# Attention, first group: the inversion in blocks of 16x16 on DVE, joined by small products on PE

## The chip, the cores and the metric

The kernel runs on one core of a Trainium2 chip. The metric is the time of one execution on the device in microseconds; of several executions the median is taken. In the text PE is TensorE (PEld its weight loads), DVE VectorE, ACT ScalarE, POOL GpSimd and SP the queue that issues most DMAs.

## The reference, cut to what matters

Three parts follow one another: a linear attention with a state, a routed feed-forward layer with eight experts, and a dense feed-forward layer. The change is in the first.

```python
for t in range(S):                              # S = 768; B, H, D = 4, 8, 40
    y[:, :, t] = einsum('bhd,bhde->bhe', rt, state)
    Sa = einsum('bhde,bhe->bhd', state, at)
    state = state * wt[:, :, None, :] - einsum('bhd,bhe->bhde', Sa, bt)
    state = state + einsum('bhd,bhe->bhde', vt, kt)
...
x = y as 3072 rows of 320
x = gate * relu(x @ w1[e]) @ w2[e]              # e: the expert with the largest logit of the row
out = g(x @ w_in) @ w_out                       # g: a leaky relu, 2048 wide
```

## The kernel before, in words

**Tiling.** Attention works in chunks of 64 steps. Inside a chunk the recurrence becomes products of matrices, once the inverse of a unit lower triangular 64x64 matrix is known, one for each chunk and head. A group is 4 chunks (256 steps) of 16 heads (two of the four batches); there are six groups. A group's 64 matrices lie as two on top of each other on the 128 partitions, for 4 chunks `c` and 8 pairs of heads `u`; the tile `l2` [128, 4, 8, 32] holds their diagonal blocks of 32x32, one in each quarter of 32 partitions, and `l1` the blocks below the diagonal.

**The inverse** (`inverse`, L529 to L614) is a generator; whoever calls `next` sets off the instructions up to the next `yield`. First DVE transposes `l2` into `ul` (L536), so that each partition holds one block of 32x32 in its free dimension: 128 blocks side by side. Then it inverts all of them by columns: for each of 31 columns `j` a product of column and row into `tmp` (L554) and a subtract from `ut` (L556), on (31-j)(j+1) elements in each partition. In the first group (`o.start`) `ut` lies in PSUM (`unit_start`) and `tmp` in SBUF; in the others `ut` lies in SBUF and `tmp` in the PSUM bank `mg`, into which ACT also copies parts of `ul` (L551). After that DVE transposes `ut` back, once as `ttc` and once as `t11` (L576, L579), and `diagonal` puts the inverted blocks on the diagonal of `tt` (L572; in the first group on DVE for the first half, else on POOL). For each half of the group (two chunks) PE then joins blocks of 32 to 64: a product of `l1` with the inverted blocks into `zp` (L600), a copy to `z` on ACT (L604), a product with `t11` into `yp` (L610), a copy with the sign into `tt` (L613). Ahead of `zp` and `yp` of the first group eight products of ones (`fill`) are issued. `zp` and `yp` take the one bank `mg`, except in the second half of the later groups. `check` (L590, L591) sums squares on ACT, with `ut` and `ttc` as the places of the unwanted output.

**Buffers.** `t4` is a ring of three tiles of 128x1024 in SBUF that all of this shares, in the order of the calls: in the first group four `junk` tiles, `ul`, `tmp`, `ttc`, `t11`; in each later one `ut` (cleared by POOL, L368), `ul`, `ttc`, `t11`. A tile that comes round again waits for the last reader of its buffer.

**Stages and order.** `prepare` (L440) loads a quarter of a group and forms two scans and a reciprocal on DVE (L467 to L469) and scaled operands (`kb`, L472; `abd`, L476); `products` (L479) multiplies them (`lp`, L497), copies `l1` and `l2` on ACT and `la` on DVE (L505); POOL at the end of each half copies parts of `l1` into `l2` (L504). `sides` (L509) transposes the operands on PE (L517, L521) with copies on ACT. `run` (L737) calls these for the first group in an order written out by hand; then come `rest` (clears), the inverse of the first group as far as the second half's checks (L805 to L807), and `prepare` and `products` of the second group. From there 48 slots follow, one for each chunk of two batches, which carry the state on, and each group's work is laid some slots ahead; the second group's inverse begins in slot 0, its matrices are needed in slot 8. Within the region of L316 the order on DVE, POOL and ACT is as written; behind it a planner chooses the order of each engine's instructions, and it always does so for PE. Each engine carries out its list in that order.

Of the kernel before, what the change touches and what calls it, by code (L numbers as in the profile page):

```python
# [9 lines left out]
F32 = mybir.dt.float32  # L10
# [5 lines left out]
ALU = mybir.AluOpType  # L16
# [4 lines left out]
P = 128  # L21
# [216 lines left out]
def whole(gen):  # L238
    for _ in gen:
        pass  # L240
# [45 lines left out]
NCS = SL // C  # L286
# [4 lines left out]
class Attention:  # L291
# [234 lines left out]
    def t4(self, nm):  # L526
        return self.pa.tile([P, NCS, 8, 32], F32, name=nm, tag="t4", bufs=3)

    def inverse(self, o):  # L529

        nc = self.nc
        l1, l2 = o.l1, o.l2
        o.tt = [self.ringed("tt", self.tt) for _ in range(2)]
        ut = self.ut0 if o.start else self.unit()
        ul = self.pa.tile([P, 32, 32], F32, name="ul", tag="t4", bufs=3)
        nc.vector.transpose(ul, l2.rearrange("p c u j -> p j (c u)"))  # L536
        yield
        for j in range(31):
            n, m = 31 - j, j + 1
            if o.start:  # L540
                if j == 0:
                    tmp = self.pa.tile([P, 1024], F32, name="tmp", tag="t4", bufs=3)
                col = ul[:, j, j + 1:]
            else:
                if j == 0:
                    bank = self.work("tmp", [P, 512], "mg")
                    tmp = bank[:, :256]
                if j in (0, 8, 16):
                    j0, j1 = j, (8, 16, 32)[j // 8]
                    part = bank[:, 256:256 + (j1 - j0) * (32 - j0)].rearrange("p (a b) -> p a b", b=32 - j0)  # L550
                    nc.scalar.copy(part, ul[:, j0:j1, j0:])  # L551
                col = part[:, j - j0, j + 1 - j0:]
            tv = tmp[:, :n * m].rearrange("p (a b) -> p a b", b=m)
            nc.vector.tensor_tensor(tv, col.unsqueeze(2).to_broadcast([P, n, m]),  # L554
                                    ut[:, j, :m].unsqueeze(1).to_broadcast([P, n, m]), op=ALU.mult)
            nc.vector.tensor_tensor(ut[:, j + 1:, :m], ut[:, j + 1:, :m], tv, op=ALU.subtract)  # L556
            if j % 2:
                yield
# [9 lines left out]
        def diagonal(half):  # L568
            for q in (1, 3, 0, 2):
                r = slice(32 * q, 32 * q + 32)  # L570
                eng = nc.vector if o.start and half == 0 else nc.gpsimd
                eng.tensor_scalar(o.tt[half][r, :, :, 32 * q:32 * q + 32], ttc[r, 2 * half:2 * half + 2], 1.0, 0.0, op0=ALU.mult, op1=ALU.add)  # L572

        vacant(0)
        ttc = self.t4("ttc")
        nc.vector.transpose(ttc.rearrange("p c u t -> p t (c u)"), ut)  # L576
        diagonal(0)
        t11 = self.t4("t11")
        nc.vector.transpose(t11.rearrange("p c u s -> p s (c u)"), ut.rearrange("p t s -> p s t"))  # L579
        yield  # L580

        pairs = [(c2, u) for u in range(8) for c2 in range(2)]
# [3 lines left out]
        for half in range(2):  # L586
            if half:
                vacant(1)
                diagonal(1)
                self.check(ut, ut, 0.01)  # L590
                self.check(l1.rearrange("p c u j -> p (c u) j"), ttc.rearrange("p c u t -> p (c u) t"), 0.01)  # L591
                yield
            tt = o.tt[half]
# [143 lines left out]
    def run(self, rt, sp, moe, ctx):  # L737
        tc, nc = self.tc, self.nc
        os = []
        for bp in range(B // 2):  # L740
            for g in range(S // SL):
                o = K()
# [42 lines left out]
        o = os[0]  # L785
# [10 lines left out]
        inv = self.inverse(o)  # L796
# [5 lines left out]
        self.count["kb"] = self.count["abd"] = 0  # L802
        with tc.issue_after(o.last_v.ins), tc.issue_after(o.last_s.ins), tc.issue_after(o.last_g.ins):
            whole(self.rest())
        for _ in range(17):  # L805
            next(inv)
        next(inv)  # L807
        self.slots_room()
        at(0, 0, lambda: whole(inv))
        with tc.issue_after(o.last_v.ins), tc.issue_after(o.last_s.ins), tc.issue_after(o.last_g.ins):  # L810
# [638 lines left out]
```

## Time and profile before

| | us |
|---|---|
| median of three runs (lowest, highest) | 1068.68 (1065.76, 1071.46) |
| the profiled execution | 1070.7 |
| its span, first to last instruction | 1068.9 |
| PE busy in the span | 972.1 |
| PEld | 867.7 |
| DVE | 682.3 |
| ACT | 537.0 |
| POOL | 479.6 |

Busy time is a mean over stages with different limits; attention ends near 470 us and the feed-forward layers fill the rest. The mean granted clock of PE was 0.965 of full speed. A chain of waits follows the work back from what ended last: each piece is released by the one before.

### The profile page before, as it was taken

To read this page: it belongs to the slowest core of one execution; us is meant where nothing else is said; L and a number is where in the kernel's file an instruction comes from. 1 tells how busy PE (TensorE), PEld (TensorE's weight loads), DVE (VectorE), ACT (ScalarE), POOL (GpSimd) and SP (SyncE) were. 2 spreads that over 40 slices of the span, in tenths; PEclk is the share of its full clock that TensorE was granted. 3 is DMA by queue.
4 is the path that set the end of the run, shared out by engine and by line. 5 is a ranking of instruction groups with operands and counts; after the bars stand their busy time and mean duration, and the time that the engine had idled before them with its cause. 6 is when DMAs were issued, how large, how long until landed. Compare 5 with 4: busy or idle time off the path is not lost.

```text
span 1068.9 us, 24462 instructions
## 1 busy us (share of the span) xinstructions
PE 972.1 (91%) x9311; PEld 867.7 (81%) x9311; DVE 682.3 (64%) x1440; ACT 537.0 (50%) x1315; POOL 479.6 (45%) x576
## 2 busy tenths in 40 slices
PE   3668988899889988888999999999999999999997
PEld 2557867787678877778999999988989988988896
DVE  8785987968869695566687776644534454444433
ACT  4556867686677868655566655521312122222211
POOL 6756687886977645420000000034334343435332
PEclk8658999999999999999999999999999999999999
DMA  4372333333333234627788865610000000100000
GB/s 122 83 230 55 90 79 86 95 76 98 91 76 87 55 71 108 184 70 230 223 266 254 258 190 177 186 41 26 25 2 25 25 25 25 26 26 25 25 1 28
DMA packets 126048, 103.34 MB, mean 97 GB/s; under 512 B 90596, under 2 KB 108004, under 8 KB 125924
## 3 DMA queue, kind: packets, MB, share of 16 engines
q1 hardware_dynamic: 122596, 89.90, 29.9%
q0 software_dynamic: 3328, 11.80, 3.5%
q8 instruction: 76, 1.25, 0.5%
q14 instruction: 48, 0.39, 0.1%
HBM read 79.39 MB, written 22.28 MB: 95 GB/s over the span
## 4 chain that ended last, share of the span: by engine, by line
PE 66%; DVE 17%; issue 5%; ACT 4%; DMA 4%; POOL 3%; SPq 0%; another core or an unknown queue 0%; POOLq 0%; DVEq 0%; ACTq 0%
PE ph L244 26%; PE po L244 24%; DVE tmp L554 3%; DVE ut L556 3%; PE lp L497 2%; DVE s L467 2%; DVE q L469 2%; PE tr_ps L272 2%; PE sa L692 2%; DVE va L697 2%; PE pp L652 2%; PE yc L708 1%; PE ap L521 1%; PE rvp L663 1%; PE xp L244 1%
## 5 line engine op out<-in xcount | busy, mean ns | idle before, releaser
L235 POOL TENSOR_TENSOR gl<-g,gh 128x512 fp32r<-128x512 f32 x96 | 123.9, 1294 | 211.0 <-ACT gh L234 120.5
L234 ACT ACTIVATE gh<-g 128x512 fp32r<-128x512 f32 x96 | 60.7, 632 | 253.0 <-DVE g L1336 174.9
L1335 DVE TENSOR_SCALAR g<-ph,al 128x512 f32<-128x512 f32 x96 | 72.1, 751 | 158.2 <-POOL gl L235 79.8
L244 PE MATMUL ph<-x2thi,win 128*128 128x512 f32 x480 | 158.8, 396 | 1.3 <-DVE g L1336 1.3
L244 PE MATMUL po<-wout,gh 128*128 128x320 f32 x768 | 138.8, 309 | 0.0
L244 PEld LDWEIGHTS po<-wout,gh 128*128 128x128 f32 x768 | 121.6, 188 | 5.7
L244 PE MATMUL ph<-x2tlo,win 128*128 128x512 f32 x288 | 114.1, 397 | 0.0
L244 PEld LDWEIGHTS ph<-x2thi,win 128*128 128x128 f32 x480 | 88.6, 188 | 16.3 <-DVE g L1336 1.8
L244 PE MATMUL ph<-xthi,we 128*128 128x448 f32 (+2 forms) x360 | 90.7, 326 | 0.0
L497 PE MATMUL lp<-kb,abd 128*128 128x128 f32 x352 | 60.3, 317 | 24.8 <-DMA wz<-in_wP_dram 8.4
L244 PE MATMUL po<-wout,gl 128*128 128x320 f32 x384 | 82.7, 311 | 0.0
L244 PE MATMUL po<-we,hh 128*128 128x320 f32 (+1 forms) x440 | 82.4, 313 | 0.3 <-ACT hh L1154 0.3
L1121 POOL DMA_DIRECT2D xe<-xs_d x16 | 10.1, 637 | 156.7 <-PE tr_ps L272 154.6
L497 PEld LDWEIGHTS lp<-kb,abd 128*128 128x128 f32 x352 | 51.1, 220 | 29.7 <-POOL abd L476 11.2
L244 PEld LDWEIGHTS po<-we,hh 128*128 128x128 f32 (+1 forms) x440 | 68.1, 181 | 2.8 <-ACT hh L1154 0.5
L244 PE MATMUL ph<-xtlo,we 128*128 128x448 f32 (+2 forms) x216 | 69.9, 325 | 0.0
L476 POOL TENSOR_TENSOR abd<-ra,q 40x512 f32<-40x512 f32 x44 | 60.5, 1375 | 19.8 <-PE ap L521 13.7
L1336 DVE SCALAR_TENSOR_TENSOR g<-ph,g 128x512 f32<-128x512 f32 x96 | 66.3, 691 | 3.1
L1154 ACT ACTIVATE hh<-ph 128x448 fp32r<-128x448 f32 (+2 forms) x70 | 31.9, 457 | 71.5 <-PE ph L244 47.7
L244 PEld LDWEIGHTS po<-wout,gl 128*128 128x128 f32 x384 | 63.9, 188 | 2.7
L692 PE MATMUL sa<-vg,pw 128*64 128x104 f32 x768 | 54.9, 260 | 12.0 <-issue 4.2
L244 PEld LDWEIGHTS ph<-xthi,we 128*128 128x128 f32 x360 | 63.0, 189 | 2.8
(227 smaller groups left out, 2306.7 us busy)
## 6 DMA issues: line engine op xcount, KB each, us to landing
raw<-in_moe_w_dram SPq DMA_DIRECT2D x16, 512.0 KB
raw<-in_moe_w_dram SPq DMA_DIRECT2D x16, 480.0 KB
kb<-in_kbP_dram SPq DMA_DIRECT2D x44, 160.0 KB
r<-in_moe_w_in_dram SPq DMA_DIRECT2D x10, 512.0 KB
r<-in_moe_w_out_dram SPq DMA_DIRECT2D x10, 512.0 KB
xs_d<-tt SPq DMA_DIRECT2D x8, 560.0 KB
raw<-in_moe_w_dram SPq DMA_DIRECT2D x16, 256.0 KB
wz<-in_wP_dram SPq DMA_DIRECT2D x48, 81.4 KB
```

The costliest lines, as they stand in the source:

```text
L234: nc.scalar.activation(hi, src, AF.Copy)
L235: return lo_eng.tensor_tensor(lo, src, f32(hi), op=ALU.subtract)
L244: return nc.tensor.matmul(out, lhsT=lhsT, rhs=rhs, start=start, stop=stop)
L272: nc.tensor.transpose(ps[:q, t:t + m], rows[:m, t // P, c * P:c * P + q], k.ident[:m, :m])
L476: nc.gpsimd.tensor_tensor(abd[r, :, q * C:(q + 1) * C], ra[r], qc[r, :, :C], op=ALU.mult)
L497: nc.tensor.matmul(lp[:, i], lhsT=abd[:, i, c2, :], rhs=kb[:, i, c2, :], start=True, stop=True)
L554: nc.vector.tensor_tensor(tv, col.unsqueeze(2).to_broadcast([P, n, m]), ut[:, j, :m].unsqueeze(1).to_broadcast([P, n, m]), op=ALU.mult)
L556: nc.vector.tensor_tensor(ut[:, j + 1:, :m], ut[:, j + 1:, :m], tv, op=ALU.subtract)
L692: nc.tensor.matmul(sa[q * 64:q * 64 + 64, i], lhsT=x.pw[:, i, q * C:(q + 1) * C], rhs=x.vg[:, i, q, :], start=True, stop=True)
L1154: self.hh_i = nc.scalar.activation(hh[:, :n], ph[:, :n], AF.Relu)
L1335: nc.vector.tensor_scalar(g, ph, 0.0, al[:, f:f + 1], op0=ALU.min, op1=ALU.mult)
L1336: g_i = nc.vector.scalar_tensor_tensor(g, ph, 0.0, g, op0=ALU.max, op1=ALU.add)
```

## The change

For the first group alone DVE inverts the two diagonal blocks of 16x16 of each block of 32x32 (`blocks`), with both blocks in one instruction of four dimensions: 15 columns instead of 31. `join` then fills the block below: PE multiplies each 32x32 block of `l2` with the right half of `ttc` (128 products, one for each chunk, pair of heads and quarter of partitions, on the tile of the array at rows and columns 32q, 16 columns wide), ACT copies the result to `spare`, PE multiplies the upper 16 rows of `t11` with that (128 products), and DVE subtracts it from `ttc`. Both sets take the bank `mg` one after the other. The first diagonal now comes behind the join, and `t11` is transposed a second time, from `ttc`. `check` reads `ttc` and writes `spare`. There are 10 calls of `next` in place of 18, as the generator has fewer pauses; the place where it stops is the same. `spare` is one more tile of the ring `t4`.

```diff
@@ -526,30 +526,63 @@
     def t4(self, nm):
         return self.pa.tile([P, NCS, 8, 32], F32, name=nm, tag="t4", bufs=3)
 
+    HB = 16
+
+    def blocks(self, ul, ut):
+
+        nc, h = self.nc, self.HB
+        both = lambda t, at, *dims: bass.AP(tensor=t.tensor, offset=t.offset + at, ap=[list(t.ap[0]), [33 * h, 2]] + [list(d) for d in dims])
+        tmp = self.pa.tile([P, 1024], F32, name="tmp", tag="t4", bufs=3)
+        for j in range(h - 1):
+            n, m = h - 1 - j, j + 1
+            tv = tmp[:, :2 * n * m].rearrange("p (k a b) -> p k a b", k=2, b=m)
+            col = both(ul, 33 * j + 1, [1, n]).unsqueeze(3).to_broadcast([P, 2, n, m])
+            nc.vector.tensor_tensor(tv, col, both(ut, 32 * j, [0, n], [1, m]), op=ALU.mult)
+            low = both(ut, 32 * j + 32, [32, n], [1, m])
+            nc.vector.tensor_tensor(low, low, tv, op=ALU.subtract)
+            if j % 2:
+                yield
+
+    def join(self, l2, ttc, t11):
+
+        nc, h = self.nc, self.HB
+        row = lambda t: t.rearrange("p c u s -> p (c u) s")
+        self.spare = self.t4("spare")
+        every = [(c, u, 32 * q) for c in range(NCS) for u in range(8) for q in range(4)]
+        zq = self.work("zq", [P, 8 * NCS, h], "mg")
+        for c, u, q in every:
+            r = slice(q, q + 32)
+            nc.tensor.matmul(zq[r, 8 * c + u], lhsT=l2[r, c, u], rhs=ttc[r, c, u, h:], start=True, stop=True)
+        nc.scalar.copy(row(self.spare)[:, :, :h], zq)
+        yq = self.work("yq", [P, 8 * NCS, h], "mg")
+        for c, u, q in every:
+            lo = slice(q, q + h)
+            nc.tensor.matmul(yq[q:q + 32, 8 * c + u], lhsT=t11[lo, c, u], rhs=self.spare[lo, c, u, :h], start=True, stop=True)
+        nc.vector.tensor_tensor(row(ttc)[:, :, h:], row(ttc)[:, :, h:], yq, op=ALU.subtract)
+
     def inverse(self, o):
 
         nc = self.nc
         l1, l2 = o.l1, o.l2
         o.tt = [self.ringed("tt", self.tt) for _ in range(2)]
+        ul = None if not o.start else self.t4("ul").rearrange("p c u j -> p (c u) j")
         ut = self.ut0 if o.start else self.unit()
-        ul = self.pa.tile([P, 32, 32], F32, name="ul", tag="t4", bufs=3)
+        if ul is None:
+            ul = self.t4("ul").rearrange("p c u j -> p (c u) j")
         nc.vector.transpose(ul, l2.rearrange("p c u j -> p j (c u)"))
         yield
-        for j in range(31):
+        if o.start:
+            yield from self.blocks(ul, ut)
+        for j in range(0 if o.start else 31):
             n, m = 31 - j, j + 1
-            if o.start:
-                if j == 0:
-                    tmp = self.pa.tile([P, 1024], F32, name="tmp", tag="t4", bufs=3)
-                col = ul[:, j, j + 1:]
-            else:
-                if j == 0:
-                    bank = self.work("tmp", [P, 512], "mg")
-                    tmp = bank[:, :256]
-                if j in (0, 8, 16):
-                    j0, j1 = j, (8, 16, 32)[j // 8]
-                    part = bank[:, 256:256 + (j1 - j0) * (32 - j0)].rearrange("p (a b) -> p a b", b=32 - j0)
-                    nc.scalar.copy(part, ul[:, j0:j1, j0:])
-                col = part[:, j - j0, j + 1 - j0:]
+            if j == 0:
+                bank = self.work("tmp", [P, 512], "mg")
+                tmp = bank[:, :256]
+            if j in (0, 8, 16):
+                j0, j1 = j, (8, 16, 32)[j // 8]
+                part = bank[:, 256:256 + (j1 - j0) * (32 - j0)].rearrange("p (a b) -> p a b", b=32 - j0)
+                nc.scalar.copy(part, ul[:, j0:j1, j0:])
+            col = part[:, j - j0, j + 1 - j0:]
             tv = tmp[:, :n * m].rearrange("p (a b) -> p a b", b=m)
             nc.vector.tensor_tensor(tv, col.unsqueeze(2).to_broadcast([P, n, m]),
                                     ut[:, j, :m].unsqueeze(1).to_broadcast([P, n, m]), op=ALU.mult)
@@ -574,9 +607,15 @@
         vacant(0)
         ttc = self.t4("ttc")
         nc.vector.transpose(ttc.rearrange("p c u t -> p t (c u)"), ut)
-        diagonal(0)
+        if not o.start:
+            diagonal(0)
         t11 = self.t4("t11")
         nc.vector.transpose(t11.rearrange("p c u s -> p s (c u)"), ut.rearrange("p t s -> p s t"))
+        row = lambda t: t.rearrange("p c u s -> p (c u) s")
+        if o.start:
+            self.join(l2, ttc, t11)
+            diagonal(0)
+            nc.vector.transpose(row(t11), row(ttc))
         yield
 
         pairs = [(c2, u) for u in range(8) for c2 in range(2)]
@@ -587,7 +626,7 @@
             if half:
                 vacant(1)
                 diagonal(1)
-                self.check(ut, ut, 0.01)
+                self.check(*((row(ttc), row(self.spare)) if o.start else (ut, ut)), 0.01)
                 self.check(l1.rearrange("p c u j -> p (c u) j"), ttc.rearrange("p c u t -> p (c u) t"), 0.01)
                 yield
             tt = o.tt[half]
@@ -802,9 +841,8 @@
         self.count["kb"] = self.count["abd"] = 0
         with tc.issue_after(o.last_v.ins), tc.issue_after(o.last_s.ins), tc.issue_after(o.last_g.ins):
             whole(self.rest())
-        for _ in range(17):
+        for _ in range(10):
             next(inv)
-        next(inv)
         self.slots_room()
         at(0, 0, lambda: whole(inv))
         with tc.issue_after(o.last_v.ins), tc.issue_after(o.last_s.ins), tc.issue_after(o.last_g.ins):
```

## Rows read from the trace of the kernel before

**Rows 1.** Page, chain of waits by line, share of the span.

```profile
PE ph L244 26%; PE po L244 24%; DVE tmp L554 3%; DVE ut L556 3%; PE lp L497 2%; DVE s L467 2%; DVE q L469 2%; PE tr_ps L272 2%; PE sa L692 2%; DVE va L697 2%; PE pp L652 2%; PE yc L708 1%; PE ap L521 1%; PE rvp L663 1%; PE xp L244 1%
```

**Rows 2.** Transpose that opens an inversion: durations ns, first and last start.

```profile
L536 DVE STREAM_TRANSPOSE ul<-l x6: 1910/2001/2041, 37.2 to 367.3; 128x1024 f32<-128x1024 f32 x6
```

**Rows 3.** Windows: length, PE, PEld, DVE, ACT, POOL busy, granted clock, DMA share, GB/s.

```profile
39.00:83.00 44.00, 29.34 (x146) 24.58 (x148) 37.77 (x83) 23.07 (x63) 30.61 (x40) 0.50 0.58 179
108.00:150.00 42.00, 38.41 (x623) 32.80 (x621) 39.47 (x113) 30.97 (x99) 30.68 (x42) 1.00 0.37 84
...
60.00:70.00 10.00, 8.17 (x39) 7.54 (x40) 8.70 (x21) 3.90 (x15) 2.35 (x2) 0.50 0.90 298
```

**Rows 4.** Chain of waits, 37 to 85 us: start, us, what.

```profile
45.85 2.58 DMA wz<-in_wP_dram
...
65.66 1.75 PE lp L497 x8
```

**Rows 5.** DVE groups, 39 to 75.36 us: busy, mean ns, idle before.

```profile
L556 DVE TENSOR_TENSOR ut<-ut,tmp 128x31 f32<-128x31 f32 (+15 forms) x31 | 10.8, 347 | 0.9
L554 DVE TENSOR_TENSOR tmp<-ul,ut 128x31 f32<-128x31 f32 (+15 forms) x31 | 10.3, 333 | 0.8
L469 DVE TENSOR_TENSOR_SCAN q<-wz,d1q 104x520 f32<-104x520 f32 x4 | 5.1, 1273 | 0.0
L467 DVE TENSOR_TENSOR_SCAN s<-wz,d1s 104x520 f32<-104x520 f32 x2 | 3.5, 1752 | 0.0
L505 DVE TENSOR_TENSOR la<-lp,negmask 128x256 f32<-128x256 f32 x4 | 1.7, 422 | 4.4 <-ACT l L499 4.4
```

**Rows 6.** DVE by form, 37 to 84 us.

```profile
L468 DVE RECIPROCAL d1q<-s 104x8 f32<-104x8 f32 x4 | 0.8, 190 | 0.0
L554 DVE TENSOR_TENSOR tmp<-ul,ut 128x135 f32<-128x135 f32 x2 | 0.6, 296 | 0.1
L556 DVE TENSOR_TENSOR ut<-ut,tmp 128x135 f32<-128x135 f32 x2 | 0.6, 293 | 0.0
L556 DVE TENSOR_TENSOR ut<-ut,tmp 128x31 f32<-128x31 f32 x2 | 0.4, 198 | 0.1
L554 DVE TENSOR_TENSOR tmp<-ul,ut 128x31 f32<-128x31 f32 x2 | 0.4, 186 | 0.1
```

**Rows 7.** Timeline 68 to 100 us, then L610 by form 37 to 96.

```profile
79.04 3.90 DVE L572 TENSOR_SCALAR tt<-ttc 32x512 f32<-32x512 f32 x4
...
82.27 1.54 PE L600 MATMUL zp<-tt,l 128*64 128x64 f32 x32
...
90.91 1.15 PE L610 MATMUL yp<-z,t 128*64 128x64 f32 x32
...
94.63 0.58 ACT L654 COPY pw<-pp 104x512 f32<-104x512 f32 x1
L610 PE MATMUL yp<-z,t 128*64 128x64 f32 x32 | 1.2, 225 | 0.0
```

**Rows 8.** Timeline around the second inversion's start; last, PE's wait for L472.

```profile
84.53 0.21 ACT L473 COPY s<-s 104x8 f32<-104x8 f32 x1 [4.38 <-DVE s L467]
...
85.28 1.08 ACT L436 ACTIVATE ttc<-l 128x1024 f32<-128x1024 f32 x1
101.40 1.30 POOL L504 TENSOR_SCALAR l<-l 32x512 f32<-32x512 f32 x2 [1.86 <-ACT l L499]
102.73 1.97 DVE L536 STREAM_TRANSPOSE ul<-l 128x1024 f32<-128x1024 f32 x1 [0.52 <-POOL l L504]
...
108.32 0.20 DVE L554 TENSOR_TENSOR tmp<-tmp,ut 128x31 f32<-128x31 f32 x1 [0.89 <-ACT tmp L551]
105.30 1.53 ACT L613 ACTIVATE tt<-yp 32x256 f32<-32x256 f32 x4 [0.25 <-PE yp L610]
...
107.90 0.38 ACT L551 COPY tmp<-ul 128x256 f32<-128x256 f32 x1
PE lp L497 <- POOL kb L472: 6.1, 1, 6.1
```


## The prediction

> **What bounds the kernel now.** I read the chain of waits first, over the whole span: half of it are the dense products of the feed-forward layers on PE (`ph` and `po`, 26% and 24%), which the change does not touch; the inversion's two lines (L554, L556) carry 3% each [rows 1]. So the question is when attention ends, and that hangs on a rhythm. The transpose that opens an inversion (`ul`) comes six times, from 37.2 to 367.3 us; without the first, which is the one changed, five from 102.7 (the second group) to 367.3, 66.1 us apart [rows 2, 8]. Each inversion needs the products of its own group and the one PSUM bank `mg` that the one before gives back. A shift of the second group's inversion should therefore move all that follows by as much, and everything from DVE's first step of it (108.32) on is taken as a fixed tail of 962 us (1070.7 less 108.3).
>
> What bounds the stretch ahead of that? By the windows, from 39 to 83 us (the first inversion up to the last diagonal) DVE is busy 37.77 of 44 us, PE 29.34 at a granted clock of 0.50 (the lower level, 1.2 GHz), ACT and POOL less [rows 3]. By engine, the chain of waits there is not DVE alone: DVE's steps to 45.85, a load of `wz`, then PE and ACT in turn (transposes L521, a clear of `tt` on ACT, the second group's products L497), and from 72 on DVE again: last steps, two transposes, the diagonals (79.04 to 82.94), a scan that ACT waits for [rows 4, 7, 8]. So DVE and PE share this stretch, and an edit that takes from one and gives to the other must be counted on both.
>
> **The change, part by part.** *Removed from DVE:* 62 steps, 10.8 + 10.3 us and 1.7 us idle in front of them [rows 5], 22.8 us in all. *Added in their place:* 15 columns with two blocks each, so 30 steps; a step's two blocks hold 2(15-j)(j+1) elements, 30 to 128, 1360 over the 15 columns (before: 5456 over 31). The forms of before give the price: 186 and 198 ns at 31 elements, 296 and 293 at 135 [rows 6]. A line through them is 153 ns + 1.06 per element for the multiply and 170 + 0.91 for the subtract: 15 x 153 + 1360 x 1.06 = 3.7 us and 15 x 170 + 1360 x 0.91 = 3.8 us, 7.5 together, with 0.03 us between steps (1.7 over 62 [rows 5]) 8.4. DVE gives back 14.4 us. The added fourth dimension of the operands has no row; I take it at nothing, and at worst 0.05 us a step, 1.5 us.
>
> *Added to DVE:* one subtract of 128x512 from PSUM (128x256 takes 0.42 us, L505 [rows 5]; at the step's slope 0.7) and a fourth 128x1024 transpose (1.9, as L536 [rows 2]). The transpose comes after the diagonals; only the second product (L610) needs it, and the first (L600) with its copies lies beside it. DVE's net relief is 11.8 us.
>
> *Added to PE:* 2 x 128 small products of 32x32 tiles with 16 columns. No row shows such a tile. The nearest are the joins of the halves: 32 products of 64 columns in 1.54 us, begun at the lower clock (48 ns each), and 32 in 1.15 at the higher (36) [rows 7]. With a quarter of the columns they will not be dearer unless the row tiles stand in each other's way; a lower end is half the warm row, 18 ns; the upper end is the mean duration of one such product, 225 ns [rows 7], if each waits for the one before. I take 48, since the stretch is at the lower clock: 6.1 us for each set, 12.3 in all (4.6 and 57.6 are the ends). Between the sets ACT copies 128x512 from PSUM, 0.6 us as L654 [rows 7]. Four handovers at about 0.25 (PE's last `lp` to ACT's copy and the like) make 1.0.
>
> *The path of the first group.* From the end of `ul` (37.2 + 1.9 = 39.1) to the end of the last diagonal (79.04 + 3.90 = 82.94) it took 43.8 us [rows 2, 7]. The first 36.2 of these, up to `ttc`, held 22.8 of steps; the other 13.4 are the second group's scans (5.1 and 3.5), `la` (1.7) and waits for ACT (4.4), which overlap in part [rows 5]. The new one: 39.1 + 8.4 of steps + 2.9 for the two scans and reciprocals already due there (1.27 and 0.19 each) + 1.9 (`ttc`) = 52.3; + 6.1 + 0.6 + 6.1 + 0.7 + 1.0 = 66.8; + 3.9 for four diagonals = 70.7 [rows 2, 5 to 7]. That would be 12.2 us early. The gain is not the steps (8.4 + 14.5 for the join against 22.8 comes to nothing): it is that DVE's other 13.4 us now lie beside PE's join and not in front of the diagonals.
>
> PE will not let all of that through. It is free for 14.7 of the 44 us [rows 3], in pieces between waits on ACT, and the join wants 12.3. I take half of it, 6.1, as paid twice (the join waits for transposes, or the second group's L497 for the join): the diagonals end at 76.8, 6.1 us early.
>
> *The second group.* Its first step (108.32) waits for ACT's copy, and that for the bank, freed by the last `tt` copy at 106.83; its own blocks were in at 102.70, its transpose done at 104.70 [rows 8]. So a bank 6 us early helps only if the products come 4 us earlier as well. What may give that: ACT waited 4.38 us (`s`, L473) for a DVE scan that stood behind the diagonals, and the second group's copies L498 stood behind it [rows 8]. With DVE ahead, that wait goes. Late next are the kb loads and POOL's L472, which held PE 6.1 us [rows 8].
>
> *Moved buffers.* `spare` is one more taker in the ring `t4`. The second group's `ul` gets the buffer of `t11`, free after the second half's L610, and no longer that of `ttc`. By the old times that is 105.3 instead of 102.7; the transpose would end at 107.2, still under the 107.90 of ACT's copy, so it costs nothing while the bank is late; without that cover 2.5 us. Behind it on DVE stand the slot's L712 to L725, for which the next slot's state waits. The second group's `ut` gets the buffer of `ttc`, free after ACT's check (85.28 to 86.36 [rows 8]); before it needed only `tmp`, done by 75.4. Behind that clear stand, on POOL, the diagonals of the second half or L472. By the old times that is up to 11 us if POOL has nothing else to do; I take 0, because the check moves up with the diagonals, and keep the rest in the slower rival. The check reads `ttc` where it read `ut` (1.0 us either way); no DMA moves, and SP's and POOL's queues keep their order. The 512 more PE instructions to load I take at nothing, beside the 179 GB/s that the stretch moves [rows 3].
>
> One rule speaks against the join. Four adjacent products write four partition quarters of one PSUM bank from four row tiles. The row of 36 ns shows two tiles of one bank side by side, but column tiles alone [rows 7]. The Trainium skill (TensorEngine Tiling (Array Packing), Restrictions and Gotchas) says that different row tiles can't access the same PSUM bank at a time. No run here shows it; taken literally it makes the set serial. What that would cost is the last rival below.
>
> *The sum.* 6 us off the profiled execution's 1070.7 (span 1068.9) is 1064.7. That execution was 2.0 above the median of the three runs, 1068.68, so I put the forecast at **1062.7**.
>
> **The rivals.** *PE takes it back* (no change): the join goes ahead of L497 and L521 of the second group, its products stay at 102.7, and the first group's slots merely start early. For: PE was busy 8.17 of 10 us from 60 to 70 [rows 3]. Against: the chain has DVE there too [rows 4], and slots that start early take their DVE work (`va`, L697) out of the stretch after 108, where DVE is busy 39.47 of 42 [rows 3]. Time: 1068.7, 1064 to 1074.
>
> *PE becomes the bound* (slower): 29.34 + 12.3 = 41.6 of 44 us at the lower clock. The join is ready at 52, ahead of the second group's first L497, and everything of that group on PE slips by it. Its `kb` loads wait for buffers that PE's own transposes free, so the 6.1 us wait for `kb` moves along instead of filling up. The last products then come 12.3 later, 115.0; with the transpose (1.97) and ACT's copy and handover (0.7) the first step is at 117.7, 9.4 late. It decides from the point where the products slip by over 2.9 us (104.70 + 0.7 against 108.32). Time: 1068.7 + 9.4 = 1078.1. For: PE at 0.50 while 82% busy from 60 to 70. Against: the idle pieces, and the ACT wait that goes [rows 3, 8].
>
> *More than I think* (faster): the higher level is granted already within the stretch; a set takes 36 ns a product [rows 7] and PE's other work shrinks too, and all 12.2 pass: 1068.7 - 12.2 = 1056.5. For: the join is two more sets in a row. Against: PE busy 82% from 60 to 70 with products and transposes stayed at 0.50 [rows 3].
>
> *The row tiles stand in line* (slower): each small product waits for the one before, 225 ns a piece: 256 x (225 - 48) = 45 us on the path, 1062.7 + 45 = 1108. For: no row shows row tiles. Against: the four quarters are disjoint partitions, and two column tiles of one bank overlap well (225 ns long, 36 apart [rows 7]). This is what the Trainium skill's rule on row tiles, above, would make of the time.
>
> **How the numbers follow.** Forecast 0.41 (its own range 1058 to 1064), more than that 0.05, PE takes it back 0.32, PE the bound 0.18, in line 0.04. One measurement of this kernel tells about 0.5% from no change, 5.3 us: 1063.4 to 1074.0. Faster 0.46 and slower 0.22 follow with no change 0.32. The range leaves out the serial tiles and the far part of either neighbour: 1054 to 1077.
>
> **What would show it.** Right: 30 steps of L554's kind at 0.19 to 0.30 us; two sets of 128 products in 4 to 7 us each between 50 and 70; diagonals that end near 77; POOL's copy into the second group's `l` near 99 and its first step near 102. If the diagonals are early but the first step is not, PE or the products took it back. If products last over 0.1 us each from start to start, the tiles are in line. If `ul` or POOL's clear of `ut` waits for PE or ACT, it is the buffers. I am wrong as a whole if the first step comes early and the end does not.

## The result: 0.9% slower

The changed kernel takes 1078.26 us (median of 5 runs, 1075.68 to 1079.41), the kernel before 1068.68 (5 runs): ratio 1.0089, 95% interval 1.0063 to 1.0115. The profiled execution took 1079.32 us, its span is 1077.6 (before 1068.9), its mean granted clock 0.962 (0.965).

### The profile after

DVE did what was asked. Its lines from 39 to 75.36 us (busy us, mean ns | idle time before; the answer to [rows 5]); L540 and L542 are the new steps, L561 the subtract behind the join:

```profile
L542 DVE TENSOR_TENSOR ut<-ut,tmp 128x30 f32<-128x30 f32 (+7 forms) x15 | 3.9, 257 | 0.4
L540 DVE TENSOR_TENSOR tmp<-ul,ut 128x30 f32<-128x30 f32 (+7 forms) x15 | 3.7, 248 | 0.5
L561 DVE TENSOR_TENSOR ttc<-ttc,yq 128x512 f32<-128x512 f32 x1 | 0.7, 687 | 8.0 <-PE yq L560 8.0
L505 DVE TENSOR_TENSOR la<-lp,negmask 128x256 f32<-128x256 f32 x1 | 0.4, 425 | 3.4 <-ACT l L499 3.4
```

8.5 us of steps instead of 22.8, but then 8.0 us of waiting for PE; the first group's diagonals on DVE end at 76.32 (82.94 before [rows 7]):

```profile
73.63 2.69 DVE L605 TENSOR_SCALAR tt<-ttc 32x512 f32<-32x512 f32 x4
```

PE's timeline there (start, us, line, xcount, idle before):

```profile
54.72 0.82 PE L555 MATMUL zq<-ttc,l 32*32 32x16 f32 x44
55.48 0.95 PE L521 MATMUL ap<-ident,tt 104*128 104x104 f32 x4
56.36 2.52 PE L555 MATMUL zq<-ttc,l 32*32 32x16 f32 x171
61.26 0.73 PE L555 MATMUL zq<-ttc,l 32*32 32x16 f32 x41 [2.37 <-issue]
61.98 2.05 PE L497 MATMUL lp<-kb,abd 128*128 128x128 f32 x8
63.82 0.90 PE L517 MATMUL bp<-ident,kb 104*128 104x104 f32 x4
64.65 0.90 PE L719 MATMUL rp<-rd,bds 128*64 128x64 f32 x12
65.48 1.04 PE L560 MATMUL yq<-spare,t 16*32 16x16 f32 x61
66.90 1.90 PE L560 MATMUL yq<-spare,t 16*32 16x16 f32 x128 [0.38 <-issue]
71.72 1.14 PE L560 MATMUL yq<-spare,t 16*32 16x16 f32 x67 [2.92 <-issue]
72.80 0.95 PE L521 MATMUL ap<-ident,abd 104*128 104x104 f32 x4
```

A product leaves two records. The 512 records are busy for 8.15 us, with 5.67 us of idle "issue" among them: time in which PE waits for nothing that the profile shows. The second group's first product (L497) starts at 61.98, its second at 73.54 (not shown above), behind the join; before the change they stood at

```profile
55.58 1.96 PE L497 MATMUL lp<-kb,abd 128*128 128x128 f32 x8
...
61.21 1.95 PE L497 MATMUL lp<-kb,abd 128*128 128x128 f32 x8
```

Its loads follow: among SP's waits from 39 to 110 us (total, times, longest; before in the first fence, after in the second) is

```profile
SPq L456 <- PE bp L517: 5.7, 4, 2.8
```

```profile
SPq L456 <- PE bp L517: 14.2, 3, 10.4
```

the `kb` loads, held by PE's transposes. So POOL's last copy into the second group's `l` and DVE's first step come late (first steps at 108.32 before [rows 8]):

```profile
107.15 1.30 POOL L504 TENSOR_SCALAR l<-l 32x512 f32<-32x512 f32 x2
```

```profile
110.98 0.20 DVE L587 TENSOR_TENSOR tmp<-tmp,ut 128x31 f32<-128x31 f32 x1
```

That is 2.7 us of the 8.7. The other 6.0 come later: from the first step to the end of the span it is 966.6 us, before the change 960.6. The first place where something is late is the end of the second group's inverse. POOL before (first fence) and after (second):

```profile
151.58 5.40 POOL L572 TENSOR_SCALAR tt<-ttc 32x512 f32<-32x512 f32 x8 [0.81 <-DVE ttc L576]
```

```profile
151.47 2.35 POOL L472 TENSOR_TENSOR kb<-kb,s 104x512 f32<-104x512 f32 x2
...
155.50 4.83 POOL L605 TENSOR_SCALAR tt<-ttc 32x512 f32<-32x512 f32 x6
160.41 2.17 POOL L504 TENSOR_SCALAR l<-l 32x512 f32<-32x512 f32 x2
162.65 2.15 POOL L605 TENSOR_SCALAR tt<-ttc 32x512 f32<-32x512 f32 x2
```

The planner has put work of the third group (L472, L504) ahead of and between the second group's diagonals. From `ttc` to the second group's first slot (slot 8; a slot's start is ACT's first copy into `va`) it takes 21.2 us instead of 15.5. The first group's slots ran 1 to 9 us early until then (slot 0 at 88.6, before 97.5; slot 7 at 144.9, 149.7) and gain nothing by it.

But the later inversions don't follow slot 8: the third group's starts only 2.1 us late (first step at 174.16, before 172.06). The step that grows is the next one. From the third group's first step to the fourth's it takes 78.0 us instead of 68.4, since the fourth group's second copy into `l` comes late on POOL, and the transpose `ul` waits for it (before in the first fence, after in the second):

```profile
233.93 1.30 POOL L504 TENSOR_SCALAR l<-l 32x512 f32<-32x512 f32 x2
```

```profile
244.09 3.24 POOL L476 TENSOR_TENSOR abd<-ra,q 40x512 f32<-40x512 f32 x2 [1.60 <-DVE q L469]
247.42 2.10 POOL L504 TENSOR_SCALAR l<-l 32x512 f32<-32x512 f32 x2
...
249.55 1.97 DVE L572 STREAM_TRANSPOSE ul<-l 128x1024 f32<-128x1024 f32 x1 [0.33 <-POOL l L504]
```

The fourth group's first step is then 11.7 us late (252.19, before 240.49); 8.7 of these are left at the end. What holds POOL's copy back there no run tests.

### The profile page after: what moved, and what is told of

Its sections match the earlier page's. It is cut to its first block, busy times and chain, and to the rows that moved or that the text cites. A ratio compares the mean times of both kernels' runs of the same rounds, so it can differ in the third digit from the quotient of the medians.

```text
span 1077.6 us, 25470 instructions
## 1 busy us (share of the span) xinstructions
PE 981.1 (91%) x9823; PEld 875.1 (81%) x9823; DVE 674.9 (63%) x1410; ACT 538.1 (50%) x1316; POOL 476.6 (44%) x576
## 4 chain that ended last, share of the span: by engine, by line
PE 63%; DVE 16%; issue 5%; POOL 5%; DMA 5%; ACT 4%; SPq 0%; POOLq 0%; DVEq 0%; ACTq 0%
PE ph L244 25%; PE po L244 24%; DVE ut L589 3%; DVE tmp L587 3%; PE lp L497 2%; PE tr_ps L272 2%; DVE q L469 2%; DVE va L736 2%; PE sa L731 1%; POOL abd L476 1%; DVE s L467 1%; PE pp L691 1%; DMA raw<-in_moe_w_dram 1%; PE ap L521 1%; POOL kb L472 1%
## 5 line engine op out<-in xcount | busy, mean ns | idle before, releaser
L244 PEld LDWEIGHTS ph<-x2thi,win 128*128 128x128 f32 x480 | 88.6, 188 | 16.4 <-DVE g L1374 1.8
L497 PE MATMUL lp<-kb,abd 128*128 128x128 f32 x352 | 57.6, 303 | 16.6 <-DMA wz<-in_wP_dram 12.0
L497 PEld LDWEIGHTS lp<-kb,abd 128*128 128x128 f32 x352 | 48.1, 207 | 20.4 <-POOL abd L476 12.8
L715 POOL TENSOR_SCALAR vg<-sm 40x160 f32<-40x160 f32 x96 | 35.2, 367 | 63.9 <-DVE sm L752 46.7
```

The source lines that it names most:

```text
L244: return nc.tensor.matmul(out, lhsT=lhsT, rhs=rhs, start=start, stop=stop)
L497: nc.tensor.matmul(lp[:, i], lhsT=abd[:, i, c2, :], rhs=kb[:, i, c2, :], start=True, stop=True)
L715: nc.gpsimd.tensor_scalar(self.by2(x.vg[C:PP, :, q, :D]), self.halves(self.sm[q * HQ:q * HQ + D, x.p2]), 1.0, 0.0, op0=ALU.mult, op1=ALU.add)
```

## Experiments

Theory 1: the join stands on PE ahead of the second group, and what it takes there comes off the second group. Theory 2: the idle "issue" in the join is slow loading of instructions while the zero fill of `xs_d` (DMAs of 560 KB each that clear a buffer of the routed layer) keeps the DMA engines at 0.91 (60 to 70 us); the queue for instructions has 4 packets from 55 to 75 us and none before the change, but 2 also in e1, which has no join. The rival to both: the planner's new order of all that follows; theory 3 (POOL's list delays the second group's diagonals) and theory 4 (the new order as a whole costs what was lost, the join little) are forms of it.

All runs in one table: ratio to the kernel before with its interval; from the timelines of each profile the second group's first step, the span less that (the "tail"), the time from the start of its `ttc` to slot 8, and the time from the third group's first step to the fourth's.

```
                             ratio   interval         first step   tail   ttc to slot 8   third to fourth
before                       1                          108.3      960.6      15.5           68.4
changed kernel               1.0089  1.0063 1.0115      111.0      966.6      21.2           78.0
 planner's own order
e1  no join                  1.0105  1.0071 1.0138      100.0      973.0      27.4           81.3
e3  early fill               1.0013  0.9993 1.0034      108.0      961.0      22.4           74.2
e3  early fill, old kernel   1.0000  0.9980 1.0019      106.2      958.2      15.4           68.4
e5  late join                1.0080  1.0053 1.0108      111.2      955.1      20.5           70.0
e6  diagonals on DVE         1.0056  1.0035 1.0078      110.2      961.8      23.9           74.3
e6  the same, old kernel     1.0086  1.0059 1.0114      106.9      967.1      24.1           72.2
e6  the same, no join        1.0038  1.0018 1.0057       99.8      974.9      26.2           78.9
e7  third group later        1.0145  1.0118 1.0171      111.5      972.1      17.4           60.7
 old order held
e9  changed kernel           1.0085  1.0052 1.0118      117.2      959.3      15.4           67.9
e12 no join                  0.9966  0.9944 0.9987      103.7      960.0      15.4           67.9
f3  half the join            1.0002  0.9979 1.0024      105.0      959.4      15.5           68.3
e14 early fill               1.0056  1.0033 1.0080      113.7      962.7      15.4           68.3
f2  yq later                 1.0027  1.0006 1.0048      110.9      962.9      15.4           69.0
f7  early fill, yq later     1.0068  1.0040 1.0096      114.1      958.0      15.4           67.8
e11 late part held           1.0045  1.0025 1.0064      111.1      958.6      15.4           68.8
f4  early fill, late held    1.0006  0.9982 1.0029      107.6      959.9      15.5           68.3
 old kernel in the new order
e16 all of it                1.0131  1.0103 1.0160      113.6      967.0      21.0           78.0
e15 late part                1.0191  1.0155 1.0227      111.7      972.4      21.4           78.0
```

The profile is one execution and need not lie at the median: e5's took 1068.05 us, its median is 1074.98; f3's took 1066.08, its median is 1071.21.

**No join (e1).** The lines of `join` are left out, but for the edit's other parts:

```diff
-        zq = self.work("zq", [P, 8 * NCS, h], "mg")
...
-        nc.vector.tensor_tensor(row(ttc)[:, :, h:], row(ttc)[:, :, h:], yq, op=ALU.subtract)
```

> Leaves out the off-diagonal 16x16 part of the first group's inverse: no zq and yq products, no copy between them, no subtract. The blocks on DVE, the buffers and the fourth transpose stay. Theory 1 (the join stands ahead of the second group's products on PE): with the join gone the second group's products are as early as before the change or earlier, POOL's second copy into its l ends at 102.7 or before (108.45 with the join), its first DVE step comes by 108.3 (110.98), and the time is 1060 to 1069. Rival (the moved buffers, or an order that the planner changed for all that follows): POOL's copy stays near 108 and the time at 1075 to 1080.

The products did come early, with the first step at 100.0, and the kernel was as slow as with the join. The rival seemed right: in this run `ttc` was done at 148.5 and POOL's diagonals began at 156.8.

**Early fill (e3), in both kernels.**

```diff
             whole(self.rest())
+            self.empty()
...
-        at(2, 0, self.empty)
```

> The changed kernel with the zero fill of xs_d issued right after the clears instead of in slot 2. Theory 2 (the join's instructions are loaded too slowly while the fill holds the DMA engines): the idle pieces in front of zq and yq (2.37, 0.38 and 2.92 us, put down to issue) shrink to under 1 us in all, the last diagonal comes near 71 instead of 76.3, the second group's products 4 to 6 us earlier than in the changed kernel, and the time is about 1072. Theory 1 (order on PE): pieces may shrink, but the products stay over 3 us later than before the change and the time stays at 1075 to 1080.

> Control for the run before it: the same move of the zero fill in the kernel before the change. It has no join, so theories 1 and 2 both expect no change: 1066 to 1072, with the second group's first step within 2 us of 108.3. If it is faster by over 5 us, the fill costs the old kernel something too, and only the difference to the changed kernel counts.

The idle pieces shrank to 1.69 and 1.73 us, products and first step came back, and most of the loss was gone; the control's time did not move (its first step came 2.1 us early). That speaks for theory 2, but not for it alone: the planner's order is another one here too.

**Late join (e5).** Two of the second group's `products` are called ahead of the join:

```diff
+        ahead = first(os[1])
+            for _ in range(2):
+                next(ahead)
```

> The changed kernel with two of the second group's eight products calls (and the loads, scans and transposes that go with them) issued ahead of the join. Theory 1: the kb loads of the third quarter are issued near 69 again (78.8 in the changed kernel), POOL's second copy into l ends near 103 instead of 108.45, the first step of the second group comes at 105 to 108.5, and the time is 1065 to 1070, though the first group's last diagonal comes later than 76.3. Theory 2 (slow loading of instructions): the same idle pieces appear wherever the join stands, and the time stays above 1074.

A miss: first step 111.2, nothing gained. The idle pieces shrank all the same, to 1.15 and 1.37 us, with the fill where it was; in this run other products stand among those of the join.

**Diagonals on DVE (e6), in three kernels; the third group a slot later (e7).**

```diff
-                eng = nc.vector if o.start and half == 0 else nc.gpsimd
+                eng = nc.vector if o.second or o.start and half == 0 else nc.gpsimd
```

```diff
-            lay(os[i], per * (i - 1))
+            lay(os[i], per * (i - 1) + (i == 2))
```

> The changed kernel with the second group's diagonals (line 605, both halves) on DVE instead of POOL. Theory 3 (POOL's list): with the first group's slots ahead, the third group's kb and l2 work stands on POOL in front of and between the second group's diagonals, and ACT's check, which writes over ttc, waits for them and holds the copies into tt. Then from ttc to the first slot of the second group it takes 15 to 17 us instead of 21.2, that slot starts near 168 (173.2), and the time is 1070 to 1075. Theory 1 alone (the join's place on PE): this stretch is no cause, the time stays at 1076 to 1080.

> Control: the same move in the kernel before the change, where POOL takes the diagonals 0.2 us after ttc is done and in one piece. Theory 3 expects no gain: 1064 to 1072, with 13 to 16 us from ttc to the first slot of the second group. If it gains over 5 us, POOL was slow there before the change too, and the run before it shows nothing on the change.

> The kernel without the 16x16 join (its products, copy and subtract are left out) and with the second group's diagonals on DVE. In the run without the join the second group's transposed block was done at 148.5, but POOL began its diagonals only at 156.8, behind products and scalings of later groups. Theory 3: without POOL the first slot of the second group comes at 160 to 166 (174), and the time at 1062 to 1070 instead of 1077.9. If the rhythm of the later inverses sets the end whatever slot 8 does, the time stays within 3 us of 1077.9.

> The changed kernel with the whole work of the third group (its loads, products and inverse) laid one slot later; nothing else. In its list POOL does the second group's eight diagonals in one piece, ahead of the third group's kb and l2 work. Theory 3: from ttc to the first slot of the second group 15 to 17 us instead of 21.2; what is gained there is lost in part at the third group (its inverse starts later), so the time is 1068 to 1076. Theory 1 alone: no change at slot 8, and 1078 or later.

Theory 3 fell. Off POOL the diagonals did not shorten the stretch (23.9 us), though that kernel's time, 1074.38, lay within the range the theory had named. e7 shortened it to 17.4, but the third group's inverse began at 184.3 (166.0) and the kernel was the slowest so far. The control taught most: in the old kernel the same small move cost 0.86%, as much as the whole change, with a tail 6.5 us longer. The diagonals take 5.6 us of DVE there, so this run doesn't separate what they cost from what the planner's new order costs; but an order that costs this much could not be ruled out any more. To judge the change, the order must be held.

**The old order held (e9), the new order in the old kernel (e16), the late part held (e11), no join in the old order (e12).** Behind `t11` both kernels emit the same instructions in the same sequence. A list of places per engine, taken from the kernel before, is turned into edges that set order alone (on all five lists; with the early fill SP's list is left to the planner):

```diff
+        for a, b in zip(want, want[1:]):
+            tc.add_manual_dep(mine[b], mine[a].name, mybir.DependencyInfo(mybir.DependencyClass.NoSync, mybir.DependencyReason.DATA), reason="hold")
```

> The changed kernel, all of its instructions as they are, but behind the first group's transpose t11 every engine's list is held in the order of the kernel before (edges that set order alone; the eight filler products stay directly ahead of zp; the join stands where the planner puts it, ahead of the second group's products on PE). Theory 4 (the planner's new order costs what was lost, the join itself little): POOL's second copy into the second group's l ends near 103 again, slot 8 comes near 165, and the time is 1060 to 1070. Theory 1 (the join's time on PE): the products are still late, that copy ends at 106 or later, and the time stays at 1074 to 1080.

> The mirror of the run above: the kernel before the change, without any of its edits, with every engine's list behind t11 held in the order that the planner gave the changed kernel. Theory 4: the old code is as slow as the new one in this order, 1074 to 1082. Theory 1: the order by itself costs little, 1066 to 1072. A part may come from POOL's second-half diagonals, which here stand ahead of the second group's scalings though the old inverse ends 25 us later: then the time is above 1082.

> The changed kernel with only the later part of the lists held in the old order (from the second group's last product on PE, its last copy into l2 on POOL and its first step on DVE); what stands ahead of that is as the planner gave it to the changed kernel. If the loss is in the early part (products 5.75 us late), the first step stays near 111 and the time is 1074 to 1079. If it is in the late part (third group's work ahead of the second group's end), from ttc to the first slot of the second group it takes 15 to 17 us and the time is 1068 to 1073.

> The kernel without the 16x16 join (products, copy and subtract left out) in the old order. It was 1077.9 in the planner's own order. Theory 4: without the join and in the old order it is the fastest of all, 1055 to 1066, and what it gains over the held changed kernel is what the join costs. If it stays above 1072, neither the join nor the order explains the loss.

In one order, the tail is nearly one number: 958.0 to 962.9 us in all eight held runs, 960.6 before; in the planner's own orders it goes from 955.1 to 974.9. The old kernel in the new order has 967.0, the changed kernel 966.6: the tail belongs to the order. So does the stretch in which it grows: from the third group to the fourth it takes 67.8 to 69.0 us in the held runs, 68.4 before, and 78.0 in the changed kernel, in e16 and in e15. And in the old order the join's cost stands bare: 1077.31 us with it, 1063.72 without. PE in e12 (first fence) and e9:

```profile
54.47 1.95 PE L497 MATMUL lp<-kb,abd 128*128 128x128 f32 x8
56.53 0.96 PE L517 MATMUL bp<-ident,kb 104*128 104x104 f32 x4
59.34 0.96 PE L521 MATMUL ap<-ident,abd 104*128 104x104 f32 x4 [1.86 <-ACT kbr L518]
60.09 1.96 PE L497 MATMUL lp<-kb,abd 128*128 128x128 f32 x8
```

```profile
61.53 0.73 PE L555 MATMUL zq<-ttc,l 32*32 32x16 f32 x41 [3.37 <-issue]
62.24 2.05 PE L497 MATMUL lp<-kb,abd 128*128 128x128 f32 x8
...
71.44 0.94 PE L560 MATMUL yq<-spare,t 16*32 16x16 f32 x55 [2.65 <-issue]
72.31 0.95 PE L521 MATMUL ap<-ident,abd 104*128 104x104 f32 x4
73.06 1.96 PE L497 MATMUL lp<-kb,abd 128*128 128x128 f32 x8
```

and POOL in e9, which has nothing to scale until PE's transpose is done:

```profile
77.26 1.17 POOL L476 TENSOR_TENSOR abd<-ra,q 40x512 f32<-40x512 f32 x1 [19.33 <-PE ap L521]
```

The second product is 13.0 us late (73.06 against 60.09), and the first step 13.5, 117.2 against 103.7. Theories 1 and 4 are both right, each for a part: the planner's early order softened the join's blow (111.0), and its late order took 6 us. e11, with the late part of the old order, gets about half of the loss back.

**What of the join costs: half of it (f3), early fill (e14), yq behind the fourth product (f2), and the late order alone (e15, f4).** The edits, all on held kernels:

```diff
-        every = [(c, u, 32 * q) for c in range(NCS) for u in range(8) for q in range(4)]
+        every = [(c, u, 32 * q) for c in range(NCS // 2) for u in range(8) for q in range(4)]
```

```diff
+            for js, at in ((zq, 0), (yq, 47)):
+                for j in js:
+                    tc.add_manual_dep(j.ins, mine[want[at]].name, mybir.DependencyInfo(mybir.DependencyClass.NoSync, mybir.DependencyReason.DATA), reason="hold")
```

> Half of the join's products on PE (two of the four chunks; the other half of the 16x16 blocks is left out), old order held. Without the join it was 1063.7 with the first step at 103.7, with all of it 1077.3 and 117.2. If the cost is what PE spends on it, ahead of the second group's products, half of it gives about half: first step near 110, time near 1070. If it is one wait that comes with any join (the bank, the copy, the subtract), the first step stays above 114 and the time above 1074.

> The changed kernel with the old order held on PE, DVE, ACT and POOL, and the zero fill of xs_d issued right after the clears. In the old order alone the idle pieces put down to issue inside zq and yq came to 6.8 us, the second group's first step to 117.2 and the time to 1077.3. Theory 2 (instructions of the join are loaded slowly under the fill): the pieces fall to 3.5 us or less, the first step to 113 or 114, the time to 1073 or 1074. If the join's cost is its busy time and its place alone, the first step stays within 1 us of 117.2.

> The whole join, old order held, but the second set (yq) stands on PE behind the second group's fourth product and its transposes, where PE waited 6.1 us for kb before the change, and no longer behind the first. Theory 1 (place on PE): products two to four come 5 to 6 us earlier than in the held run (73.1, 77.0, 80.3), the fifth before 87 (89.3), the first step at 110 to 114 and the time at 1069 to 1074, although the first group's last diagonal comes later. If only the sum of PE's work counts, nothing changes: 117 and 1077.

> The whole change with the early zero fill, in the planner's own order up to the second group's first step, and from there on in the old order. With the early fill the first step came at 108.0 (before the change 108.3), but the planner's later order cost 6.7 us at the second group's first slot. If order is what remains: slot 8 at 164 to 166, the time at 1064 to 1068, as before the change or a little less. If the later loss has another cause it stays at 1069.

> The kernel before the change, its early part as it was, with the lists held in the changed kernel's order only from the second group's last product and first step on. If the planner's later order costs by itself, the first step stays at 106 to 110, the first slot of the second group comes 3 us or more later than 164.9, and the time is 1.004 to 1.007 of the kernel before. If the later order costs only where the work ahead of it is late as well, the ratio is 0.998 to 1.003.

> The whole change, with the three mends together: the old order held on PE, DVE, ACT and POOL, the second set of the join behind the second group's fourth product, the zero fill right after the clears. The split place alone was 1.0027 of the kernel before, the early fill took 3.5 us of first step in the held order. If both add up: first step at 106 to 108, ratio 0.997 to 1.001. If the join's 8 us of PE time can't be placed for nothing, it stays above 1.002.

Half the join costs 1.3 us of first step, the whole 13.5, so less than its share. By the ratios it is 0.36% and 1.19%, and there the intervals don't tell 0.36% from one half. The sets of half the join run without an idle piece, here the second one in f3:

```profile
59.69 1.91 PE L560 MATMUL yq<-spare,t 16*32 16x16 f32 x128
61.53 0.95 PE L521 MATMUL ap<-ident,abd 104*128 104x104 f32 x4
62.27 1.96 PE L497 MATMUL lp<-kb,abd 128*128 128x128 f32 x8
```

The second product is 2.2 us late, though the join is busy for 4 us: PE's free pieces swallow the rest. With all of it the idle pieces come to 6.8 us (e9). The early fill takes them to 3.0 and the first step back by 3.5; a later `yq` by 6.35. Both moved the first step as was expected of them (e14's time, 1076.69, lay above the 1073 to 1074 expected, beside 1069.87 for the kernel before), and together they don't (f7, a miss): with the fill ahead of the second group's loads in the held order, POOL waits 8.1 us for `kb` and PE's first product starts at 59.3. f4 ends where the kernel before does (1070.38, above the 1064 to 1068 expected, beside 1069.87 for the kernel before). Its slot 8 came at 164.5, in e3 at 171.6, and the two ratios are the same within their intervals: a late slot 8 by itself need not cost anything. No version with the whole join beat the kernel before. e15 was a miss too (first step 111.7, expected by 110; ratio 1.0191, expected up to 1.007). Its tail is 11.8 us longer than that of the same kernel in its own order, but 7.0 of these lie inside the second group's inverse (first step to `ttc` 48.1 us, 41.1 in the kernel before and in e16), which the new order as a whole doesn't lengthen. That the order costs without a join is shown by e16, its size by e16 and e11.

## Why the prediction was wrong

It said 1062.7 within 1054 to 1077 and faster; it was slower, and just outside. By its own steps:

- *DVE's steps* (8.4 us, `ttc` ready at 52.3): 8.5 and 52.2. Right.
- *The join's price* (6.1 us a set, last diagonal at 76.8): the diagonal came at 76.32, but by luck, as two errors cancel. The 48 ns were those of a record, of which a product leaves two (the x32 of [rows 7] are 16 products), so the count was half of what it had to be; and a record of the small tile takes 14.7 ns of busy time (171 in 2.52 us), 8.15 us in all and not 12.3. Against that the 5.67 us of "issue" have no term in it, and all loading was taken at nothing ("The 512 more PE instructions to load"). The row tiles don't stand in line. The Trainium skill (TensorEngine Tiling (Array Packing), Restrictions and Gotchas) holds that different row tiles can't access the same PSUM bank at a time. The trace doesn't agree: the records of four row tiles go to one bank, on disjoint partitions, and start 13.6 ns apart on the mean (2.52 us less the last record's 0.21, over 170), while each lasts 210 ns; the measurement decides.
- *The second group* is the step that failed. Its products were to come 4 us earlier, because ACT's wait for DVE goes. That gain is real: without the join, in the old order, POOL's copy ends at 98.06 and not 102.70, 4.6 us early, for 0.34% of the time. But what the join takes of PE was charged to the first group's diagonals alone, and to these products at nothing. PE carries out its list in order, the join's data is ready ahead of theirs, and so they pay: 13.5 us in the old order. In the changed kernel they were 5.75 late. The bank, freed at 99.53 instead of 106.83, was no longer what they waited for.
- *The fixed tail* failed as well. It is fixed within 5 us (958 to 963; 960.6 before by the span, 962 in the prediction by the execution's time) as long as each engine's list keeps its order. The planner made new lists, and that cost 6.0 of the 8.7 us; the forecast had no term for it. The sign that it named for being wrong as a whole, an early first step without an early end, is what e1 shows: 100.0 and 1077.89.
- *The buffers* cost nothing: `ul` starts 0.03 us after POOL's copy, `ut` is cleared at 76.84.

The rival "PE becomes the bound" had the mechanism, and 1078.1 for the time: the products slip and drag the `kb` loads along. In the old order it came out as written (first step 117.2, forecast 117.7), though its 12.3 us rest on the same two errors. In the changed kernel it gave only 2.7 us; that its time was hit to 0.2 us owes the rest to the order. That the late order costs is shown (e11, e16), and in which stretch (from the third group's inverse to the fourth's); which of its many moved instructions cost most is not: the one that was tried, the diagonals on POOL, was not it. That the idle pieces are loading of instructions is argued, from f3 and from the early fill, and not shown: the packets tell little, since e1 has some too, and in e5 the pieces shrank without the early fill.

## What to carry to other kernels

Work that is moved to another engine is paid by whatever stands behind it in that engine's list, not only by what waits for its result: look at who is next in line, and at who waits for that one. Where a planner orders the instructions, a local edit is a global one: the old kernel, with no other edit, lost 1.3% in the changed kernel's order (e16). Hold the order, or run the old kernel in the new one, before a difference of that size is put down to the edit.

## What the runs showed of the hardware

- Small products on 32x32 tiles with 16 columns take 14.7 ns of busy time a record at the granted clock of 0.50 (1.2 GHz), less than a third of the 48 ns a record of the joins with 64 columns [rows 7], and 13.6 ns from start to start, while each lasts 210 (mean ns in the row; starts are recorded, ends modelled). So they overlap, on four row tiles in one bank.

```profile
L555 PE MATMUL zq<-ttc,l 32*32 32x16 f32 x256 | 4.1, 210 | 2.4 <-issue 2.4
```

- In the runs with the whole join the idle pieces come after about the same number of records (`zq` stops after 213 to 215 in the changed kernel and in e3, e9, e14, f2 and f7, and after 202 in e5, where 16 other records stand among them); sets of 128 have none.
- From 60 to 70 us PE is busy 6.48 us at 0.50 with the join (e9, first fence), 8.22 us at a mean of 0.72 without (e12). No run ties this to the join: the kernel before has none, and PE is busy 8.17 us there at 0.50 [rows 3]. Eight `lp` records first take 1.08 us, and no longer 1.96, at 80.3 in e9 and at 67.0 in e12.

```profile
60.00:70.00 10.00, 6.48 (x254) 6.01 (x254) 3.02 (x4) 1.44 (x4) 0.00 (x0) 0.50 0.93 308
```

```profile
60.00:70.00 10.00, 8.22 (x50) 7.31 (x48) 3.35 (x6) 4.83 (x18) 3.56 (x4) 0.72 0.91 309
```
